# Decode attention with an MLP gate: TensorE in two two-round loops, w1 and V0 between the K halves, wide strip matmuls for the MLP output and three wo groups

## Chip, cores, metric

One Trainium2 chip, one core. The metric is device microseconds of one execution, lower is better. Each ratio below is the mean time of one kernel's fast runs over the mean of the other kernel's fast runs of the same rounds, so it is not quite the ratio of the medians that stand beside it. For a one-core kernel a run counts as "slow" when it is over 1.5% above the fastest run of the same kernel in the same comparison; the medians in the tables take in such runs, the ratios do not.

## The reference

Four batches, one token each, D = 512, 32 query heads in 8 groups, a cache of which the last 1024 positions count.

```python
def _A_ref(x, k_cache, v_cache, wq, wo):            # attention
    q = (x @ wq) -> (B, 32, 1, 128)
    k, v = last W = 1024 rows of the caches, each of 8 groups used by 4 heads
    p = softmax(q k^T * Dh**-0.5);  o = p v
    return o.reshape(B, 1, 4096) @ wo
def _B_ref(x, w1, b1, w2, b2):                      # MLP, 512 -> 1792 -> 512
    return gelu(layernorm(x) @ w1 + b1) @ w2 + b2

xn = layernorm(x)
s  = _A_ref(xn, k_cache, v_cache, wq, wo)
g  = silu(_B_ref(xn, w1, b1, w2, b2))
return x + s * g                                    # bf16 inputs and output
```

(Shortened. The weights and caches are some 28.8 MB, read once.)

## The kernel before

Each of the 8 K groups (1 MB) is transposed on TensorE in four units of eight 128x128 tiles, copied to SBUF by VectorE, and multiplied with q. V follows, group by group, then the product with wo. All TensorE code is written out: there is no loop. Loads go through SyncE in program order, and a load into a used slot waits for the last reader of that slot.

```python
NS, LAG, NKT, NB = 8, 8, 10, 3
d_wq = [load_wq(0)]; load_k(0); load_k(1); d_wq.append(load_wq(1))
for g in range(2, HKV): load_k(g)                   # kv_buf has 8 slots: all of K fits
...
def load_v(g):                                      # V goes into the slots of K
    dma(kv_buf[:, (HKV + g) % NS], cache_rows(A_v_cache, g), t_last[(HKV + g) % NS])
...
for n in range(LAG, NUN + LAG):                     # NUN = 32 units
    if n < NUN: T(n)                                # 8 transposes, copy to kt_buf
    S(n - LAG)                                      # 8 score matmuls, exp after the 4th
load_v(0); d_w1 = ...; load_v(1); d_w2 = ...
for g in range(HKV):
    if g >= 2: load_v(g)
    if g == 4: d_wox = ...                          # 128 rows of wo in a freed part of wq_sb
    PV(g)                                           # 32 matmuls and one for the denominator
    if g == 0: epilogue(0); mlp1()
    if g >= 2: epilogue(g - 1)
    if g == 1: mlp2(); mlp3()                       # MLP output: 56 narrow matmuls, early
    if g == 2: mlp4()
epilogue(HKV - 1)
... load_wo in pieces of 1 MB, 1, 1, 0.5, 0.25, 0.125

def wo(tiles, *deps):                               # "narrow": weights are 128x128 of wo,
    for w, o, st, sp in tiles:                      # the moving side has 4 columns
        for c in range(4):
            pe.matmul(psM[:, PS_W + c*4 : PS_W + (c+1)*4], w[:, c*128:(c+1)*128], o, ...)
rows = to_rows()
wo(wox...); for each wo piece: wo(...); gate; transpose; add x; store
```

The softmax here doesn't subtract the row's maximum and nothing guards it: scores larger than these inputs give would overflow.

Of the kernel before, what the change touches and what calls it, by code (L numbers as in the profile page):

```python
# [4 lines left out]
class _Op:  # L5
    __slots__ = ("eng", "fn", "deps", "sem", "count", "used")

    def __init__(self, eng, fn, deps, sem=None):
        self.eng = eng
        self.fn = fn  # L10
        self.deps = [d for d in deps if d is not None]
        self.sem = sem
        self.count = 0
        self.used = False


class _Program:



    ENGS = ("pe", "dve", "act", "gp", "sp")

    def __init__(self, nc):
        self.nc = nc
        self.ops = {e: [] for e in self.ENGS}
        self.sems = {e: nc.alloc_semaphore("e_" + e) for e in self.ENGS}

    def add(self, eng, fn, *deps):
        op = _Op(eng, fn, deps)
        self.ops[eng].append(op)  # L30
        return op

    def dma(self, eng, name, fn, *deps):
        op = _Op(eng, fn, deps, sem=self.nc.alloc_semaphore("d_" + name))
        self.ops[eng].append(op)
        return op

    def plan(self):
        for e in self.ENGS:
            for op in self.ops[e]:  # L40
                for d in op.deps:
                    if d.eng != e or e != "pe":
                        d.used = True
        for e in self.ENGS:
            n = 0
            for op in self.ops[e]:
                if op.sem is None:
                    if op.used:
                        n += 1
                    op.count = n  # L50

    def emit(self, e, engine):
        seen = {}
        for op in self.ops[e]:
            need = {}
            for d in op.deps:
                if d.sem is not None:
                    need[d.sem.name] = (d.sem, 16)
                elif d.eng != e or e != "pe":
                    s = self.sems[d.eng]  # L60
                    if need.get(s.name, (s, 0))[1] < d.count:
                        need[s.name] = (s, d.count)
            for name, (s, v) in need.items():
                if seen.get(name, 0) < v:
                    engine.wait_ge(s, v)
                    seen[name] = v
            last = op.fn(engine)
            if op.sem is not None:
                last.then_inc(op.sem, 16)
            elif op.used:  # L70
                last.then_inc(self.sems[e], 1)


def bass_recurrent_scan__sliding_block_cached__mixer_channel_mlp__decode_kernel(
# [20 lines left out]
    B, D = 4, 512  # L95
# [10 lines left out]
    NS = 8  # L106
    LAG = 8
    NKT = LAG + 2
# [17 lines left out]
    wox_sb = wq_sb[0:44, 0, 0:6 * D].rearrange("p (j o) -> p j o", j=6)  # L126
# [24 lines left out]
    ident32 = sb([128, 128], F32)  # L151
    ind = sb([128, 128], BF16)
# [6 lines left out]
    qT = sb([128, 128], BF16)  # L159
# [5 lines left out]
    selx = sb([128, 6, 44], BF16)  # L165
    OW3 = sb([128, 12], BF16)
    OWx = sb([44, 24], BF16)
# [18 lines left out]
    pg = _Program(nc)  # L186
# [18 lines left out]
    def load_k(g):  # L205
        d_k[g] = pg.dma("sp", "k%d" % g, lambda e: e.dma_start(
            kv_buf[:, g, :, :].rearrange("p c d -> p (c d)"), cache_rows(A_k_cache, g)),
            )

    def load_v(g):  # L210
        d_v[g] = pg.dma("sp", "v%d" % g, lambda e: e.dma_start(  # L211
            kv_buf[:, (HKV + g) % NS, :, :].rearrange("p c d -> p (c d)"), cache_rows(A_v_cache, g)),
            t_last[(HKV + g) % NS] if HKV + g >= NS else None)

# [6 lines left out]
    d_wq = [load_wq(0)]  # L221
    load_k(0)
    load_k(1)
    d_wq.append(load_wq(1))
    for g in range(2, HKV):
        load_k(g)
# [30 lines left out]
    c_sx = add("gp", lambda e: e.memset(selx[:, :, :], 0.0))  # L257
    for h in range(2):
        c_sx = add("gp", lambda e, h=h: e.affine_select(
            selx[:, 0:5, 32 * h:32 * h + 12], ones_bf[:, 0:60], [[1, 5], [5, 3], [15, 4]],  # L260
            ALU.is_equal, 0.0, base=60 * h, channel_multiplier=-1), c_1, c_sx)
    c_sx5 = add("gp", lambda e: e.affine_select(
        selx[:, 5, 0:8], ones_bf[:, 0:8], [[1, 8]], ALU.is_equal, 0.0,
        base=120, channel_multiplier=-1), c_1, c_sx)
# [22 lines left out]
    cp = {}  # L287
    sc = {}
    ex = [None] * HKV
    den = [None] * HKV  # L290
    ep = [None] * HKV

    def T(n):
        g, u = n // NU, n % NU

        def fn(pe):
            last = None
            for j in range(UT):
                last = pe.transpose(psK[n % NB][:, j * 128:(j + 1) * 128],  # L299
                                    kv_buf[:, g, u * UT + j, :], ident[:, :])  # L300
            return last
        t = add("pe", fn, d_k[g], c_id, cp.get(n - NB), v_xyT if n >= LAG else None)
        if u == NU - 1:
            t_last[g] = t
        cp[n] = add("dve", lambda e: e.tensor_copy(kt_buf[:, n % NKT, :], psK[n % NB][:, 0:1024]),  # L305
                    t, sc.get(n - NKT))

    def S(n):
        g, u = n // NU, n % NU

        def fn(pe):
            last = None
            if u == 0:
                pe.matmul(psS[g % 2][:, 0:512], ind[:, :], negm[:, :], start=True, stop=False,  # L314
                          skip_group_check=True)
            for j in range(UT):
                c = u * UT + j
                last = pe.matmul(psS[g % 2][:, c * 16:(c + 1) * 16],  # L318
                                 kt_buf[:, n % NKT, j * 128:(j + 1) * 128],
                                 qT[:, g * 16:(g + 1) * 16],  # L320
                                 start=False, stop=(c == NC - 1), skip_group_check=True)
            return last
        sc[n] = add("pe", fn, cp[n], v_q, c_neg, c_ind,
                    ex[g - 2] if u == 0 and g >= 2 else None)
        if u == NU - 1:
            ex[g] = add("act", lambda e: e.activation(  # L326
                P_buf[:, g, :], psS[g % 2][:, 0:512], AF.Exp, scale=SCALE),
                sc[n])

    def PV(g):  # L330
        pso = psO[g % 2]

        def fn(pe):
            last = None
            for c in range(NC):
                last = pe.matmul(pso[:, 0:16], kv_buf[:, (HKV + g) % NS, c, :],  # L336
                                 P_buf[:, g, c * 16:(c + 1) * 16],
                                 start=(c == 0), stop=(c == NC - 1))
            return last
        pv_op[g] = add("pe", fn, ex[g], d_v[g], ep[g - 2] if g >= 2 else None)  # L340

        den[g] = add("pe", lambda pe: pe.matmul(psS[g % 2][:, 0:512], ones_bf[:, :], P_buf[:, g, :],  # L342
                                                start=True, stop=True),
                     ex[HKV - 2 + g % 2], ep[g - 2] if g >= 2 else None)

    def epilogue(g):
# [9 lines left out]
            pso[:, 0:16], rden[:, cs], ALU.mult), v, pv_op[g])  # L356


    v_xyT = None
    for n in range(LAG):  # L360
        T(n)

    def f_xy(pe):
        last = None
        for s, src in ((0, xn_bf), (16, y_bf)):
            for c in range(4):
                last = pe.transpose(psK[1][:, s + c * 4:s + c * 4 + 4],  # L367
                                    bass.AP(src, c, [[512, 4], [4, 128]]), ident[0:4, 0:4])
        return last
    t_xy = add("pe", f_xy, v_xn, v_y, c_id, cp[LAG - 1])  # L370

    v_xT = add("dve", lambda e: e.tensor_copy(
        xT[:, :, 0:4], psK[1][:, 0:16].rearrange("p (c b) -> p c b", c=4)), t_xy, c_xT)
    v_xyT = add("dve", lambda e: e.tensor_copy(
        yT[:, :, 0:4], psK[1][:, 16:32].rearrange("p (c b) -> p c b", c=4)), t_xy, c_yT)
# [16 lines left out]
    def f_qT(pe):  # L392
        last = None
        for k in range(8):
            last = pe.transpose(psK[1][:, k * 128:(k + 1) * 128],  # L395
# [4 lines left out]
    for k in range(2):  # L400
        v_q = add("dve", lambda e, k=k: e.tensor_copy(
            bass.AP(qT, k * 64, [[128, 128], [16, 4], [4, 4], [1, 4]]),
            bass.AP(psK[1], k * 512, [[1024, 128], [32, 4], [1, 4], [128, 4]])), t_qT)
# [6 lines left out]
    def f32k(n):  # L410

        return kt_buf[:, n, 0:2 * FS].bitcast(F32)
    hb = kt_buf[:, 4, 0:FS]
    h_ps = psK[0][:, 0:2 * FS].bitcast(F32)

    def mlp1():
# [12 lines left out]
        t = add("pe", fn, v_xyT, d_w1, d_b1, *[cp[n] for n in range(NUN - NB, NUN)])  # L429
# [17 lines left out]
    def mlp3():  # L447
        def fn(pe):
            last = pe.matmul(psM[:, PS_Z:PS_Z + 16], b2_sb[:, :],  # L449
                             bass.AP(ident, 0, [[128, 4], [1, 4], [0, 4]]),  # L450
                             start=True, stop=False, skip_group_check=True)
            for k in range(FC):
                for c in range(4):
                    last = pe.matmul(psM[:, PS_Z + c * 4:PS_Z + (c + 1) * 4],
                                     w2_sb[:, k, c * 128:(c + 1) * 128], hT[:, k, 0:4],
                                     start=False, stop=(k == FC - 1), skip_group_check=True)
            return last
        t = add("pe", fn, mlp["h"], d_w2, d_b2, c_id)
# [9 lines left out]
    NUN = HKV * NU  # L468
    for n in range(LAG, NUN + LAG):
        if n < NUN:  # L470
            T(n)
        S(n - LAG)
    load_v(0)
    d_w1 = pg.dma("sp", "w1", lambda e: e.dma_start(
        w1_sb[:, :, :], B_w1.rearrange("(p c) f -> p c f", c=4)))
    load_v(1)
    d_w2 = pg.dma("sp", "w2", lambda e: e.dma_start(
        w2_sb[:, :, :], B_w2.rearrange("(p c) o -> p c o", c=FC)))
    for g in range(HKV):
        if g >= 2:  # L480
            load_v(g)
        if g == 4:


            R3 = (7 * 512 + 384) * D
            d_wox = [pg.dma("sp", "wox%d" % h, lambda e, h=h: e.dma_start(
                wox_sb[32 * h:32 * h + 12, 0:5, :].rearrange("p j o -> p (j o)"),
                bass.AP(A_wo.tensor, R3 + 60 * h * D, [[5 * D, 3], [15 * D, 4], [1, 5 * D]])),
                t_q) for h in range(2)]
            d_wox.append(pg.dma("sp", "wox2", lambda e: e.dma_start(  # L490
# [143 lines left out]
```

## Time and profile before

| | before |
|---|---|
| time, median of 3 | 76.88 us (76.87 to 76.88) |
| profiled span | 75.0 us |
| last V load lands | 62.22 us |
| last wo load lands | 71.89 us |
| TensorE's last narrow matmul ends | 72.22 us |
| 16 KB instruction fetches of TensorE | 8 |

The table of windows cuts the span in stages: window, its length, busy time of each engine (PE, PEld, DVE, ACT, POOL) with its instructions, the clock granted to TensorE, the DMA share, and GB/s. Of the kernel before:

```profile
33.00:47.00 14.00, 11.69 (x270) 9.53 (x269) 7.79 (x13) 2.99 (x5) 0.00 (x0) 0.94 1.00 423
47.00:63.00 16.00, 11.30 (x289) 8.24 (x287) 10.82 (x24) 1.31 (x3) 0.00 (x0) 0.50 1.01 423
```

The last column is what to read: 423 GB/s in both stages, with every other engine idle part of the time. The DMA sets the time until the last wo piece lands, and TensorE finishes 0.33 us after it. So a change must leave the queue fed and TensorE's tail under the last landing, or it costs time.

### The profile page before, as it was taken

The numbers are of one execution on the slowest core, as the hardware profiler recorded it, in microseconds if no ns is written. First come the engines' busy times: TensorE is split into PE (matmuls) and PEld (weight loads), VectorE is DVE, ScalarE is ACT, GpSimd is POOL, SyncE is SP. The second block draws the span as 40 slices with busy tenths as digits, with TensorE's granted clock in tenths as the row PEclk, the third lists the DMA queues.
The fourth block names the chain that finished last, engine by engine and source line by source line (L and its number), as shares of the span: only waits on it lengthen the run. The fifth ranks groups of instructions, "written<-read, shape, count | busy, mean of one in ns | idle before, by whom it ended". The sixth has DMA issues, their size and how long they took to land.

```text
span 75.0 us, 2384 instructions
## 1 busy us (share of the span) xinstructions
PE 49.1 (66%) x1089; PEld 40.3 (54%) x1089; DVE 41.2 (55%) x84; ACT 9.7 (13%) x16; POOL 7.2 (10%) x19
## 2 busy tenths in 40 slices
PE   0000029965689999959979937910899977379670
PEld 0000029953279989959979902500886555268640
DVE  0778106894258989959977060269639774620020
ACT  0611000000270320303203600230000000000000
POOL 6999300000000000000000000000000000000000
PEclk9999999999999999999999995555555555555555
DMA  1999999998999999999999999999999999999800
GB/s 37 271 413 420 417 420 476 437 420 376 433 437 433 415 433 420 424 415 464 419 398 425 461 413 401 424 420 428 419 429 428 420 409 420 417 411 419 322 25 2
DMA packets 4266, 28.99 MB, mean 387 GB/s; under 512 B 508, under 2 KB 648, under 8 KB 1697
## 3 DMA queue, kind: packets, MB, share of 16 engines
q1 hardware_dynamic: 4206, 28.84, 92.6%
q8 instruction: 8, 0.13, 0.6%
q10 hardware_dynamic: 50, 0.01, 0.1%
q14 instruction: 2, 0.01, 0.0%
HBM read 28.85 MB, written 0.00 MB: 385 GB/s over the span
## 4 chain that ended last, share of the span: by engine, by line
DMA 39%; PE 34%; SPq 15%; DVE 5%; issue 3%
DMA wo_sb<-in_A_wo_dram 26%; PE psK L299 20%; SPq L510 14%; DMA kv_buf<-in_A_k_cache_dram 13%; PE psS L318 6%; DVE kt_buf L305 4%; PE psO L383 3%; PE psS L314 2%; PE psM L555 2%; DVE q_sb L389 1%; PE psK L395 1%; PE psK L367 1%; PE psS L576 1%; SPq L218 1%; SPq L211 0%
## 5 line engine op out<-in xcount | busy, mean ns | idle before, releaser
L299 PE MATMUL psK<-ident,kv_buf 128*128 128x128 bf16 x256 | 20.5, 231 | 11.9 <-DMA kv_buf<-in_A_k_cache_dram 10.7
L305 DVE COPY kt_buf<-psK 128x1024 bf16<-128x1024 bf16 x32 | 21.1, 691 | 7.4 <-PE psK L299 7.3
L299 PEld LDWEIGHTS psK<-ident,kv_buf 128*128 128x128 bf16 x256 | 16.3, 104 | 11.3 <-DMA kv_buf<-in_A_k_cache_dram 10.7
L318 PEld LDWEIGHTS psS<-qT,kt_buf 128*128 128x128 bf16 x256 | 9.4, 96 | 2.1 <-issue 1.2
L318 PE MATMUL psS<-qT,kt_buf 128*128 128x16 bf16 x256 | 10.4, 169 | 0.2 <-issue 0.2
L336 PEld LDWEIGHTS psO<-P_buf,kv_buf 128*128 128x128 bf16 x256 | 7.5, 103 | 3.4 <-DMA kv_buf<-in_A_v_cache_dram 1.8
L336 PE MATMUL psO<-P_buf,kv_buf 128*128 128x16 bf16 x256 | 8.0, 174 | 0.9 <-DVE den_sb L349 0.7
L349 DVE TENSOR_REDUCE den_sb<-psS 128x16 f32<-128x512 f32 x8 | 5.5, 687 | 5.1 <-PE psS L342 4.9
L326 ACT ACTIVATE P_buf<-psS 128x512 bf16<-128x512 f32 x8 | 4.8, 597 | 16.2 <-PE psS L318 16.2
L555 PE MATMUL psM<-OW,wo_sb 128*128 128x4 bf16 x124 | 4.1, 167 | 0.8 <-DMA wo_sb<-in_A_wo_dram 0.8
L342 PE MATMUL psS<-P_buf,ones_bf 128*128 128x512 bf16 x8 | 4.5, 561 | 0.0
L555 PEld LDWEIGHTS psM<-OW,wo_sb 128*128 128x128 bf16 x124 | 3.7, 105 | 1.1 <-DMA wo_sb<-in_A_wo_dram 0.9
L572 DVE TENSOR_TENSOR sg_sb<-psM,g_sb 128x16 f32<-128x16 f32 x1 | 0.2, 185 | 5.8 <-PE psM L555 5.8
L421 PE MATMUL psK<-w_sb,yT 128*32 128x448 bf16 x16 | 2.0, 561 | 1.8 <-issue 1.8
L314 PE MATMUL psS<-negm,ind 128*128 128x512 bf16 x8 | 3.0, 380 | 0.0
L449 PE MATMUL psM<-ident,b_sb 4*128 4x16 bf16 x1 | 0.2, 190 | 3.8 <-DVE hT L444 3.8
L431 DVE SCALAR_TENSOR_TENSOR kt_buf<-kt_buf,psK 128x448 f32<-128x448 f32 x1 | 0.6, 622 | 3.7 <-ACT kt_buf L430 3.7
L449 PEld LDWEIGHTS psM<-ident,b_sb 4*128 4x128 bf16 x1 | 0.1, 99 | 4.3 <-DVE hT L444 4.3
L390 ACT ACTIVATE q_sb<-psO 128x512 bf16<-128x512 f32 x1 | 0.6, 597 | 13.1 <-PE psO L383 13.1
L267 DVE CAST P_buf<-x_bf 4x512 f32<-4x512 bf16 x1 | 1.0, 956 | 2.2 <-DMA x_bf<-in_A_x_dram 2.2
L352 DVE RECIPROCAL rden<-den_sb 128x16 f32<-128x16 f32 x8 | 2.0, 253 | 0.3
L440 DVE TENSOR_TENSOR kt_buf<-kt_buf,psK 128x448 bf16<-128x448 f32 x1 | 2.1, 2083 | 0.0
(74 smaller groups left out, 36.0 us busy)
## 6 DMA issues: line engine op xcount, KB each, us to landing
kv_buf<-in_A_k_cache_dram SPq DMA_DIRECT2D x8, 1024.0 KB, 20.6
kv_buf<-in_A_v_cache_dram SPq DMA_DIRECT2D x8, 1024.0 KB, 24.0
wq_sb<-in_A_wq_dram SPq DMA_DIRECT2D x2, 2048.0 KB, 11.4
w_sb<-in_B_w_dram SPq DMA_DIRECT2D x2, 1792.0 KB, 28.3
wo_sb<-in_A_wo_dram SPq DMA_DIRECT2D x3, 1024.0 KB, 24.0
wo_sb<-in_A_wo_dram SPq DMA_DIRECT2D x1, 512.0 KB, 19.6
wo_sb<-in_A_wo_dram SPq DMA_DIRECT2D x1, 256.0 KB, 16.4
wo_sb<-in_A_wo_dram SPq DMA_DIRECT2D x1, 128.0 KB, 14.6
```

What stands on the lines that cost most here:

```text
L299: last = pe.transpose(psK[n % NB][:, j * 128:(j + 1) * 128], kv_buf[:, g, u * UT + j, :], ident[:, :])
L305: cp[n] = add("dve", lambda e: e.tensor_copy(kt_buf[:, n % NKT, :], psK[n % NB][:, 0:1024]), t, sc.get(n - NKT))
L314: pe.matmul(psS[g % 2][:, 0:512], ind[:, :], negm[:, :], start=True, stop=False, skip_group_check=True)
L318: last = pe.matmul(psS[g % 2][:, c * 16:(c + 1) * 16], kt_buf[:, n % NKT, j * 128:(j + 1) * 128], qT[:, g * 16:(g + 1) * 16], start=False, ...
L326: ex[g] = add("act", lambda e: e.activation(P_buf[:, g, :], psS[g % 2][:, 0:512], AF.Exp, scale=SCALE), sc[n])
L336: last = pe.matmul(pso[:, 0:16], kv_buf[:, (HKV + g) % NS, c, :], P_buf[:, g, c * 16:(c + 1) * 16], start=(c == 0), stop=(c == NC - 1))
L342: den[g] = add("pe", lambda pe: pe.matmul(psS[g % 2][:, 0:512], ones_bf[:, :], P_buf[:, g, :], start=True, stop=True), ex[HKV - 2 + g % 2] ...
L349: v = add("dve", lambda e: e.tensor_reduce(den_sb[:, cs], bass.AP(psS[g % 2], 0, [[512, 128], [1, 16], [16, NC]]), AX.X, ALU.add), den[g])
L383: last = pe.matmul(psO[m // 4][32 * s:32 * s + 32, 0:512], xT[:, c, :], wq_sb[:, c, m * 512:(m + 1) * 512], start=(c == 0), stop=(c == 3), ...
L440: v = add("dve", lambda e: e.tensor_tensor(bass.AP(kt_buf, 4 * UT * 128, [[NKT * UT * 128, 128], [1, 32], [32, FC]]), f32k(3).rearrange("p ...
L510: d_wo.append((g0, g1, i0, i1, pg.dma("sp", "wo%d" % n, lambda e: e.dma_start(wo_sb[:, g0:g1, i0:i1, :], wo_r[:, g0:g1, i0:i1, :]))))
L555: last = pe.matmul(psM[:, PS_W + c * 4:PS_W + (c + 1) * 4], w[:, c * 128:(c + 1) * 128], o, start=(st and c == 0), stop=sp, skip_group_che ...
```

## The change

The intent: TensorE's written-out code is about 2,290 instructions, by an estimate nine blocks: the trace before shows fetches of 16 KB, and between its first four stalls for them lie 127 or 128 matmuls with as many weight loads, so some 256 instructions a block. The fetches move beside the data: after the first, at 24.3 us, fifteen increments of a K load came by 25.32 us and the sixteenth at 26.48. Two hardware loops of two rounds each, 4 K groups a round and 4 V groups a round, and wide matmuls in the tail bring it to about 1,330. In a loop of this program both rounds use the same slots, semaphores and buffers, hence the rest: K uses slots 0 to 3 twice, V slots 4 to 7 twice, w1 and V0 are loaded between the K halves, the softmax weights of groups 4 to 7 are copied into those of 0 to 3 by ScalarE, and the MLP output stands after the V loop.

```diff
-    d_wq = [load_wq(0)]
-    load_k(0)
-    load_k(1)
-    d_wq.append(load_wq(1))
-    for g in range(2, HKV):
+    d_wq = [load_wq(0), load_wq(1)]
+    for g in range(NG):                                    # NG = 4
         load_k(g)
 ...
     def load_v(g):
-            kv_buf[:, (HKV + g) % NS, ...], cache_rows(A_v_cache, g)),
-            t_last[(HKV + g) % NS] if HKV + g >= NS else None)
+            kv_buf[:, NG + g % NG, ...], cache_rows(A_v_cache, g)),
+            pv_op[g - NG] if g >= NG else None, sem=d_v[g - NG].sem if g >= NG else None)
 ...
+                with pe.Fori(0, 2, 1):                      # K loop and V loop
+                    for op in ops: ...
+    for r in range(2):
+        pg.seg = ("k", r)
+        if r:
+            d_w1 = ...
+            load_v(0)
+            for g in range(NG, HKV):
+                load_k(g)
+        for n in range(RU + LAG): ...                       # RU = 16, LAG = 3
+    load_v(1); d_w2 = ...; load_v(2); load_v(3)
+    mlp1()
     for g in range(HKV):
-        if g >= 2:
+        pg.seg = ("v", g // NG)
+        if g >= NG:
             load_v(g)
         PV(g)
+        epilogue(g)
 ...
-            for k in range(FC):                             # MLP output: 56 narrow matmuls
-                for c in range(4): ...
+            for k in range(FC):                             # 14 wide ones on four strips
+                i, m = k % 4, 32 if k < 4 else 4
+                last = pe.matmul(psK[1][32 * i:32 * i + m, ...], hT[:, k, 0:m],
+                                 w2_sb[:, k, :], ..., tile_position=(0, 32 * i))
+        mlp["zc"] = add("act", lambda e: e.activation(f32r(5), z_ps, AF.Copy), t)
+    def folded(pe, src, o, first, last):                    # sums the strips, and transposes
+        for c in range(4):
+            r = pe.matmul(psM[:, o + c * 4:o + (c + 1) * 4], src[:, c * 128:(c + 1) * 128],
+                          fold[:, :], ...)                  # src and fold are FP32
 ...
     rows = to_rows()
-    wo(wox: 6 tiles) ; wo(groups 0 to 6)
+    mlp3b()                                                 # fold of the MLP output
+    mlp4()
+    wide(groups 0 to 2: 12 matmuls of 512 columns); wide(wox: 2)
+    w_c = add("act", lambda e: e.activation(f32r(6), psK[2][...], AF.Copy), t_w)
+    add("pe", lambda pe: folded(pe, f32r(6), PS_W, True, False), w_c, c_fold, mlp["g"])
+    wo(groups 3 to 6)
```

(Not in this excerpt: the bookkeeping of semaphores that a loop needs; the layout of the extra 128 wo rows, "wox", which changes from 40 KB on three DMA engines to 16 KB on eight, which the traces show as three data increments in each of its two large transfers before and eight after; wo pieces of 1.5, 1, 0.5, 0.5, 0.25 and 0.125 MB.)

## The prediction

> **What bounds the kernel now.** I read the page first (busy shares, slices, queues), then the chain of work that ended last, the timeline of the tail, the timeline around TensorE's "issue" gaps, and last the trace's record of when each of a DMA's sixteen increments arrived. The page's slices and queues:
>
> ```profile
> PE   0000029965689999959979937910899977379670
> PEclk9999999999999999999999995555555555555555
> DMA  1999999998999999999999999999999999999800
> GB/s 37 271 413 420 417 420 476 437 420 376 433 437 433 415 433 420 424 415 464 419 398 425 461 413 401 424 420 428 419 429 428 420 409 420 417 411 419 322 25 2
> ...
> q1 hardware_dynamic: 4206, 28.84, 92.6%
> q8 instruction: 8, 0.13, 0.6%
> ```
>
> The DMA row is 9 from the second slice to the 38th at about 420 GB/s, while TensorE has gaps. 28.84 MB must be moved, and neither kernel moves fewer data bytes. The clock row says that TensorE has half its clock from about 45 us on. The chain of work that ended last says the same of its second half:
>
> ```profile
> 51.25 0.04 issue
> 51.30 19.64 DMA wo_sb<-in_A_wo_dram
> 70.93 0.05 issue
> 70.98 0.59 PE psM L555 x16
> 71.57 0.04 issue
> 71.61 0.61 PE psM L555 x12
> 72.22 0.02 issue
> 72.24 0.20 DVE sg_sb L572
> ```
>
> The last 28 narrow matmuls run as the last wo pieces land (71.89 us is the last increment); then come 3.1 us of product, transpose, sum and output to the end at 75.0. The timeline of the tail shows how little room TensorE has there:
>
> ```profile
> 66.51 0.88 PE L555 MATMUL psM<-OWx,wq_sb 44*128 44x4 bf16 x24 [0.53 <-DVE OWx L547]
> 67.33 1.87 PE L555 MATMUL psM<-OW,wo_sb 128*128 128x4 bf16 x64
> 69.73 1.01 PE L555 MATMUL psM<-OW,wo_sb 128*128 128x4 bf16 x32 [0.54 <-DMA wo_sb<-in_A_wo_dram]
> 70.98 1.23 PE L555 MATMUL psM<-OW,wo_sb 128*128 128x4 bf16 x28 [0.23 <-DMA wo_sb<-in_A_wo_dram]
> ```
>
> Its waits for DMA there are 0.54 + 0.23 = 0.77 us: TensorE may grow by about 0.8 us after 66.5 before it, and not DMA, sets the end.
>
> The second reading is of **instruction fetches**. In the trace eight 16 KB packets of the instruction queue start at 24.3, 30.8, 36.8, 43.0, 49.2, 57.7, 64.9 and 70.1 us, each taking 0.88 to 0.97 us. TensorE stops for "issue" soon after the first four:
>
> ```profile
> 33.08 0.22 PE L299 MATMUL psK<-ident,kv_buf 128*128 128x128 bf16 x1 [0.81 <-issue]
> 45.48 0.56 PE L421 MATMUL psK<-w_sb,yT 128*32 128x448 bf16 x4 [1.81 <-issue]
> ```
>
> These gaps lie 127 matmuls apart, which with their weight loads and a wait or two is 256 instructions = 16 KB. Each ends 1.3 to 1.5 us after the packet, and the next packet starts 3.7 to 4.2 us after the gap. So one block is fetched ahead, only once the block before it is entered, and it takes about 4 + 0.95 + 1.35 = 6.3 us under this load. That costs TensorE some 3.3 us in the K stage, but the bytes flow on.
>
> A fetch also delays one of the sixteen DMA engines by 1.2 to 1.4 us to the end. The fifth K load got fifteen increments by 25.32 us, the sixteenth at 26.48; every fetch up to the seventh adds one late engine. The last wo piece has five increments at 70.25 to 70.57, one at 71.05, ten at 71.53 to 71.89 (seven with a fetch, and the three engines that carry 40 KB each of the extra wo rows: those two transfers show three data increments each); the mean is 71.29. **Perfect balance is worth 0.6 us, no fetches at all about 1.3.** Two per cent of 76.88 is 1.54.
>
> [...] no line of this trace shows whether old blocks stay usable. [...] The change hangs on which holds. [...] the 32 q matmuls of 128x512 take 1.91 us, 60 ns each at full clock. [...] The change adds FP32 matmuls with 128-column weights; the kernel before has one such only with 16 columns.
>
> **The change part by part.**
>
> Loops. Sixteen units of transpose and score are 260 matmuls, 520 instructions, some 535 with waits: over two blocks. V: 4 x 33 matmuls, some 280 instructions. With the narrower tail TensorE's code falls from about 2,290 to about 1,330 instructions, nine blocks to six. If old blocks stay, fetches fall from eight to about five: 0.05 MB, 0.1 us of DMA on average. But the last engine still has one fetch on it, so the last landing moves only 0.1 or 0.2 us. The V copies on ACT (8 x 0.6 us at most; ACT is 13% busy) and the register work lie beside.
>
> DMA order. wq entire first: its second half lands at 13.1 instead of 18.0; K3 at 22.9; w1 and V0 (2.9 MB at 0.43 MB a us) hold 6.9 us; K4 lands at 32.2, K7 at 39.7. After V1, w2, V2, V3 and the wox rows, the queue is fed until about 51.9, so V4 must be issued by about 50, and it now waits for V0's products. Transpose plus score takes 0.65 us a unit (2.8 us a group). Starting at 32.2 and half cold, the second K round ends at 44 to 45, w1 products at 46.5, V0's at 48: in time by 2 us. No gain, as the bytes are the same.
>
> Tail. V7 lands at about 62.1 as before, and its products end at 63.7. Then, at half clock: 14 strip matmuls for the MLP. Four of 448 columns took 0.37 us a round (L421), so 512 columns 0.43; four rounds with drain 1.7, of which 1.3 lie beside the epilogue on DVE (to 65.0): 65.3. Row products 0.8: 66.1. Fold of the MLP, four FP32 matmuls and a bias: I estimate 0.3 us each, from the one FP32 transpose here that took 383 ns against about 220 for bf16: 1.3, so 67.4. Wide matmuls for three groups and wox, four rounds plus drain: 1.9, so 69.3. ACT copy 0.6 with a hand-over of 0.1: 70.0. Second fold 1.2: 71.2. Groups 3 to 6, 64 narrow ones at 29 ns: 1.9. Last 12: 0.4 and drain. End about 73.6, against 72.24 before: **+1.3 us**. It removes 24 + 48 narrow ones, 2.1 us, but puts two folds, a copy and wide ones in the chain. With folds half as dear, or TensorE warm, it ends with the DMA at 72.1.
>
> Sum where old blocks stay: -0.1 for DMA, 0 to +1.3 for the tail: 76.8 to 78.1.
>
> **The rivals.**
>
> Old blocks do not stay [...]. Then the K loop's back branch waits 6.3 us for its first block and again for following ones, and the V loop too: 12 or 13 fetches. The 6.9 us of w1 and V0 would hide the first stall; that they stand just there speaks for the author expecting one. But the first block has only about 80 body instructions, 2 us of work, so another 4 us wait follows, then over 1 us per block. K would end at 50 to 54, V0's products at 55 or later, and V4 would be issued 4 us after the queue ran dry. The V back branch would put another 6 to 12 us in front of V4's products. That makes 80 to 88 us. For it: the gaps before, a fetch on demand each time. Against it: [...] that a loop would save no fetch then. I give it a third.
>
> Balance. If fetches vanish or avoid the engines that carry wox (now 16 KB on eight engines, 0.6 us, instead of 40 KB on three), the last landing comes up to 1.0 us earlier: 75.9. If they hit the same engines, 0.5 later. It cannot reach 2%.
>
> TensorE warm in the tail: then +0. Before, it stayed at half clock from 45 us with 7 tenths busy, which speaks against.
>
> **Range and chances.** About two thirds on 76.0 to 78.5, centred a little above the present time; a third on 80 and beyond, wide. The median of that mixture is about 77.4 us. 76.0 to 83.0 leaves a twentieth below and some 15% above. Faster by over 2%: 0.04, as no term reaches 1.54 us. Slower: nearly all of the third and a little of the rest, 0.36. Within: 0.60.
>
> **What would show it.** Right: the instruction queue with about five packets; no "issue" gap of over 1 us at the start of the second K and V rounds; DMA row at 9 to the 38th slice; last wo increment at 71.5 to 72.0; TensorE's last narrow matmuls without waits for DMA, later than 72.24. [...] I am wrong if the last landing comes a full 1.5 us earlier, if FP32 folds take over 0.6 us each, or if a wait on a slot (V4 on V0's products) starves the queue without any fetch gap.

## The result, and the profile after

The changed kernel is slower. In the first comparison it took 79.95 us median (78.76, 79.58, 80.33 and 81.27; the latter two count as slow) against 76.88; ratio of fast runs 1.0294, interval 1.0201 to 1.0387. In a later one it took 80.59 (80.25 to 81.0, six runs, all fast) against 76.80; ratio 1.0501, interval 1.0475 to 1.0526. The profile below is that of the 78.76 us run. It is the fastest run, for a reason that its clock row shows. Its page:

```profile
PEclk9999999999999999965999999999555555598555
GB/s 36 248 419 426 470 452 358 422 434 434 417 476 395 409 441 400 443 422 426 422 434 433 463 400 411 430 329 374 396 405 417 415 407 422 422 413 399 116 9 2
q8 instruction: 5, 0.08, 0.4%
PE psM L561 4%; PE psM L670 3%; PE psK L552 2%; PE psK L683 1%; PE psO L426 1%; ACT kt_buf L697 1%; ACT kt_buf L557 1%; PE psS L433 1%; PE psS L712 1%; DVE o_bf L714 0%; DVE sg_sb L708 0%; PE psM L567 0%
```

Five fetches instead of eight (q8). A dip in the GB/s row, 329 374 396, in the middle of the V stage. And a chain that ended last (fourth line) with no DMA in it, as far back as it is followed (to 63.36 us): before, wo's DMA stood in it until 70.93 us. The clock row has "98" in slices 36 and 37 of 40: in this run TensorE got its full clock for one stretch of 3.4 us, from 67.2 us on.

**The loops fetch once.** The fetches begin at 23.0, 29.1, 51.3, 68.4 and 73.8 us: two in the first K round, none in the second, though a round has 128 transposes and 128 score matmuls, each with a weight load, which are 512 instructions without the waits; one in the first V round, none in the second. The back edge costs a branch of 0.22 us (0.08 where not taken), in the trace's records of the K and of the V loop. The timeline has a gap at the start of the second K round, and its releaser is TensorE's sequencer:

```profile
33.60 3.32 PE L387 MATMUL psK<-ident,kv_buf 128*128 128x128 bf16 x32 [4.10 <-PEq L99]
```

It is no fetch. The last increment of K4 arrived at 33.47, 0.13 us before; the wait for it is given to the instruction of the loop that waits. Fourteen of K4's sixteen increments were there by 32.08, the last two came at 33.46 and 33.47. After the first fetch one increment of w1 came late (28.60, the others by 27.17), after the second two of V0 (31.03 and 31.18, the others by 29.64), and two of each load from K4 to V1. So the two fetches of the first K round seem to start the second one 1.4 us later; this is read from the increments, and no run tests it.

**A hole before V4.** TensorE and SyncE around it, the timeline first, then the waits of the DMA queue (line waited for: us in total, times, longest):

```profile
47.26 0.94 PE L518 MATMUL psK<-w_sb,yT 128*32 128x448 bf16 x16 [0.78 <-ACT P_buf L415]
48.13 0.37 PE L522 MATMUL psK<-b_sb,ones_bf 1*32 1x448 bf16 x4
48.43 1.99 PE L426 MATMUL psO<-P_buf,kv_buf 128*128 128x16 bf16 x64
...
56.22 0.94 PE L426 MATMUL psO<-P_buf,kv_buf 128*128 128x16 bf16 x29 [2.21 <-DVE OTb L448]
```

```profile
SPq L294 <- PE psO L426: 17.6, 2, 16.4
```

V4's load waits in SyncE for V0's products (L426), and is issued at 49.42 us, when those 32 matmuls end. The queue had V3 (increments from 50.72 to 52.38) and wox (51.07 to 53.40) left, unevenly over its engines. The trace's packet records, which no view prints, show the hole: from about 50.4 us engines stand empty, between 50.5 and 51.0 some 11 of the sixteen are busy and move 0.27 MB a us, and V4's first packets start at 50.88, 1.5 us after the issue. The rate is back above 0.42 MB a us only at 58, though most engines are busy by then; why it stays low so long is not shown. V4's first increment arrives at 54.16, its last at 55.82, 4.74 and 6.40 us after the issue. TensorE then waits 2.2 us for V4 (the page names VectorE, which came last by its record; V4's last increment at 55.82 is what fits). The windows give the loss:

```profile
33.00:47.00 14.00, 12.66 (x256) 12.26 (x260) 10.57 (x16) 2.28 (x4) 0.00 (x0) 0.88 1.01 427
47.00:63.00 16.00, 9.08 (x247) 6.98 (x251) 10.47 (x23) 3.53 (x7) 0.00 (x0) 0.71 0.98 398
```

398 against 423 GB/s over 16 us is 0.40 MB, or 0.95 us. V7's last increment is at 63.27 us instead of 62.22, wo's at 73.18 instead of 71.89.

How late V4 is issued goes with the clock of the second K round, in which TensorE is busy for over 12 of 14 us. In the window from 33 to 47 us the mean granted clock is 0.88 here and in the profiles of e1, e5 and e11, and V4 is issued at 49.42 to 49.58 us; in those of e2, e3, e4 and e6 it is 0.79 to 0.82, and V4 is issued at 50.04 to 50.36. V7 then lands at 62.90 to 63.62 us in the first four and at 63.99 to 64.28 in the others. That of e3, to set beside the first line above:

```profile
33.00:47.00 14.00, 13.35 (x256) 12.68 (x257) 10.67 (x16) 1.79 (x3) 0.00 (x0) 0.81 1.01 428
```

**A longer tail.** The timeline of TensorE in the tail, from the profile of the later comparison (80.95 us, half clock throughout the tail):

```profile
65.29 1.89 PE L552 MATMUL psK<-w_sb,hT 128*32 128x512 bf16 x14
66.67 0.62 PE L644 MATMUL psS<-OTb,sel 128*32 128x28 bf16 x16
...
68.00 1.87 PE L561 MATMUL psM<-fold,kt_buf 128*128 128x4 f32 x8
69.80 1.47 PE L683 MATMUL psK<-wo_sb,OW 128*32 128x512 bf16 x12
71.20 0.59 PE L683 MATMUL psK<-wq_sb,OWx 64*4 64x512 bf16 x2
72.47 1.87 PE L561 MATMUL psM<-fold,kt_buf 128*128 128x4 f32 x8 [0.69 <-ACT kt_buf L697]
74.20 2.17 PE L670 MATMUL psM<-OW,wo_sb 128*128 128x4 bf16 x76
```

wo's last increment is at 73.27 us here. TensorE ends at 76.37, 3.1 us after it, and nothing in this list waits for DMA. Each fold (L561), four FP32 matmuls in the program, stands as eight pairs of weight load and matmul and takes 1.87 us; such a weight load took a median of 333 ns here, against 106 in e11, where the folds are BF16. In the 78.76 us run the same lines are 1.06, 0.83, 0.38 and 1.71 us:

```profile
67.63 1.06 PE L561 MATMUL psM<-fold,kt_buf 128*128 128x4 f32 x8
68.61 0.83 PE L683 MATMUL psK<-wo_sb,OW 128*32 128x512 bf16 x12
69.38 0.38 PE L683 MATMUL psK<-wq_sb,OWx 64*4 64x512 bf16 x2
70.44 1.71 PE L561 MATMUL psM<-fold,kt_buf 128*128 128x4 f32 x8 [0.69 <-ACT kt_buf L697]
```

So the tail of this kernel is TensorE's and moves with the clock, and it spreads from 78.8 to 81.3 us, where the kernel before, whose tail is the DMA's, stays at 76.7 to 77.0. Of its ten runs in both comparisons the two with the highest mean clock (0.848 and 0.845) are the two fastest (78.76 and 79.58 us); the other eight, at 0.786 to 0.821, are not in the order of their clocks. The profiles show two places where the clock acts, this stretch of 3.4 us and the second K round; which of them made each run is not on record.

### The profile page after: what moved, and what is told of

It reads as the page before. It is cut to its first block, busy times and chain, and to the rows that moved or that the text cites. A ratio compares the mean times of both kernels' runs of the same rounds, so it can differ in the third digit from the quotient of the medians.

```text
span 76.9 us, 2253 instructions
## 1 busy us (share of the span) xinstructions
PE 49.6 (64%) x989; PEld 40.8 (53%) x1001; DVE 40.4 (53%) x85; ACT 13.1 (17%) x22; POOL 7.6 (10%) x23
## 5 line engine op out<-in xcount | busy, mean ns | idle before, releaser
L387 PEld LDWEIGHTS psK<-ident,kv_buf 128*128 128x128 bf16 x256 | 17.3, 108 | 4.2 <-issue 4.2
L426 PE MATMUL psO<-P_buf,kv_buf 128*128 128x16 bf16 x256 | 7.9, 172 | 7.2 <-PEq L99 4.7
L426 PEld LDWEIGHTS psO<-P_buf,kv_buf 128*128 128x128 bf16 x256 | 7.3, 100 | 8.8 <-issue 4.6
L407 PE MATMUL psS<-qR,kt_buf 128*128 128x16 bf16 x256 | 10.5, 170 | 0.4
L407 PEld LDWEIGHTS psS<-qR,kt_buf 128*128 128x128 bf16 x256 | 9.6, 96 | 1.1
L475 PE MATMUL psO<-wq_sb,xT 128*32 128x512 bf16 x32 | 3.8, 628 | 2.9 <-DMA wq_sb<-in_A_wq_dram 2.7
L481 DVE CAST q_sb<-psO 128x512 bf16<-128x512 f32 x1 | 0.7, 691 | 6.5 <-PE psO L475 6.5
L475 PEld LDWEIGHTS psO<-wq_sb,xT 128*32 128x32 bf16 x32 | 0.9, 129 | 5.0 <-DMA wq_sb<-in_A_wq_dram 3.6
L561 PE MATMUL psM<-fold,kt_buf 128*128 128x4 f32 x16 | 2.8, 296 | 0.7 <-ACT kt_buf L697 0.7
L561 PEld LDWEIGHTS psM<-fold,kt_buf 128*128 128x128 f32 x16 | 2.6, 247 | 1.0 <-ACT kt_buf L697 1.0
L437 ACT ACTIVATE P_buf<-P_buf 128x512 bf16<-128x512 bf16 x4 | 2.4, 621 | 2.0 <-PE psS L433 1.3
L670 PEld LDWEIGHTS psM<-OW,wo_sb 128*128 128x128 bf16 x76 | 2.3, 106 | 0.0
```

Of the source, the lines that this page charges most:

```text
L387: last = pe.transpose(psK[n % NB][:, j * 128:(j + 1) * 128], kv_buf[:, lg, u * UT + j, :], ident[:, :])
L407: last = pe.matmul(psS[lg % 2][:, c * 16:(c + 1) * 16], kt_buf[:, n % NKT, j * 128:(j + 1) * 128], qR[:, lg * 16:(lg + 1) * 16], start=Fal ...
L426: last = pe.matmul(pso[:, 0:16], kv_buf[:, NG + lg, c, :], P_buf[:, lg, c * 16:(c + 1) * 16], start=(c == 0), stop=(c == NC - 1))
L437: pc[lg] = add("act", lambda e: e.activation(P_buf[:, lg, :], P_buf[:, NG + lg, :], AF.Copy), den[g], cls="pc")
L475: last = pe.matmul(psO[m // 4][32 * s:32 * s + 32, 0:512], xT[:, c, :], wq_sb[:, c, m * 512:(m + 1) * 512], start=(c == 0), stop=(c == 3), ...
L561: r = pe.matmul(psM[:, o + c * 4:o + (c + 1) * 4], src[:, c * 128:(c + 1) * 128], fold[:, :], start=first and c == 0, stop=last, skip_grou ...
```

## The experiments

The theory: two things cost time, the late issue of V4 (a hole in the DMA) and the FP32 folds in TensorE's tail; the loops themselves cost and gain nothing. Rivals: the loops (branches, waits, semaphore work) cost it; the loss is all DMA; the loss is elsewhere in the order of loads. All kernels gave correct results. Slow by the 1.5% rule were three of the four runs of e2, one of six in e5 and in e6, and two of six in e11.

| run | median us (range, runs) | before beside it | ratio, 95% interval |
|---|---|---|---|
| e1 the change, again | 80.59 (80.25–81.0, 6) | 76.80 | 1.0501, 1.0475–1.0526 |
| e2 loops written out | 81.03 (79.11–81.16, 4) | 76.80 | none (one fast run) |
| e3 wide wo undone | 78.55 (78.27–79.38, 6) | 76.80 | 1.0248, 1.0210–1.0286 |
| e4 a wo piece ahead of V4 | 81.21 (81.1–81.45, 4) | 76.80 | 1.0578, 1.0560–1.0596 |
| e5 both wide forms undone | 78.37 (77.79–78.97, 6) | 76.83 | 1.0198, 1.0157–1.0238 |
| e6 e5 with a wo piece ahead | 78.32 (77.73–79.78, 6) | 76.83 | 1.0156, 1.0126–1.0186 |
| e7 V4–V7 in K's slots | 79.27 (79.18–80.33, 6) | 76.83 | 1.0341, 1.0298–1.0384 |
| e8 the K loop alone | 77.31 (77.07–77.6, 6) | 76.83 | 1.0068, 1.0049–1.0087 |
| e9 before, with wide wo | 77.88 (77.86–78.76, 5) | 76.80 | 1.0152, 1.0128–1.0175 |
| e10 e8, wox laid out as before | 76.74 (76.62–76.89, 6) | 76.80 | 0.9989, 0.9974–1.0004 |
| e11 folds in BF16 | 78.49 (78.11–80.02, 6) | 76.80 | 1.0199, 1.0168–1.0230 |
| e12 e7 with folds in BF16 | 77.14 (76.73–77.24, 6) | 76.80 | 1.0033, 1.0011–1.0055 |

e1 to e4 ran on one chip, e5 to e8 on a second, e9 to e12 on a third. Across those, only the ratios to the kernel before are compared.

### e1: the changed kernel again

No edit.

> The changed kernel unaltered, as a control. Theory A: the 2 to 4 us that it loses come from two places, (1) V4 waits for the slot that V0's products free, so the DMA queue runs dry for about 1 us at 50 to 54 us, and (2) a serial TensorE chain after V7 lands (11 us: products, MLP strips, row products, fold, wide wo, copy, fold, 76 narrow matmuls) that outlasts the DMA. Both depend on the TensorE clock, [...] so the time spreads from run to run: 78.7 to 81.5 us, while the kernel before stays within 76.8 to 77.1 on the same chip. Rival (noise of the earlier chip): this one repeats within 0.3% too.

Measured 80.59 us, ratio 1.0501. All six runs lie within 0.75 us, where the slower half of the first comparison lies too, so 80 to 81 us is read as this kernel's usual time and the 78.76 us run as the exception. This is the tail shown above.

### e2: the same order with the loops written out

```diff
-            if not isinstance(seg, tuple):
+            if True:                                        # no loop; own semaphores for K4-7, V4-7
                 for op in ops:
```

> The changed kernel with TensorE's two loops written out straight, each transfer with its own semaphore, nothing else changed. Theory A (the loops themselves are harmless, and spare fetches): no gain, 78.7 to 82 us, with about 7 or 8 packets in the instruction queue in place of 5, issue gaps in the K stage again, and V4 issued no earlier than 49.4 us, rather 1 to 2 us later. Rival B (branches, semaphore lowering or refetched blocks of the loops cost the time): 77.5 us or less and the tail as short as before.

Measured 81.03 us. Three of four runs are at 81.0 to 81.2, with a mean clock of 0.785 to 0.802, and one at 79.11 with 0.846. The profile, which by the 1.5% rule counts as slow beside that one run, has eight fetches again; V4 is issued at 50.24 us, TensorE's folds take 1.87 us each, and wo lands at 73.92. With one fast run there is no verdict; but no run came near the 77.5 us of the rival, and the late V4 and the long tail are there without loops. So nothing here says that the loops cost the time, and three fetches fewer do not show as a gain either. For the K loop e10 is the firmer test; the V loop has no other than this.

### e3: wide matmuls for wo undone

```diff
-    wide(groups 0 to 2); t_w = wide(wox); w_c = copy; folded(w_c)
-    for g0, g1, i0, i1, d in d_wo[1:]:
+    wo(wox: 2 tiles)
+    for g0, g1, i0, i1, d in d_wo:                          # all groups narrow
```

> The changed kernel with the wide wo matmuls, their copy and the second fold undone: all of wo in narrow matmuls, MLP output still in strips with its fold. Theory A: the stretch from the first wide matmul to the start of the 76 narrow ones (68.6 to 72.2, 3.55 us) becomes 56 narrow ones at 29 ns (1.6 us), so the chain is about 1.9 us shorter and the DMA sets the end again: last wo increment near 73.2, TensorE done 0.35 us later, 0.7 us off the profiled run and more off the slow ones: 77.8 to 78.4 us, and less spread. Rival C (the tail is set by DMA, the wide form lies beside it): no change, 78.7 to 80.

Measured 78.55 us, ratio 1.0248 against 1.0501 of the unaltered change on the same chip: 2.0 us gained by undoing one wide form, with more matmuls (124 narrow ones instead of 76, and 8 for wox). In its profile V4 was issued at 50.20 us and V7 landed at 64.18, later than in e1 (the slower second K round shown above), and it is still faster. The wide form with its copy and fold is a loss where TensorE is the tail.

### e4: a wo piece issued ahead of V4

```diff
+        if g == NG:
+            load_wo(2, 5, 6, 0, 4)                          # 512 KB that wait for no slot
         if g >= NG:
             load_v(g)
```

> The changed kernel with one 512 KB piece of wo (group 5) issued ahead of V4, so that it fills the hole in the queue. Theory A: the GB/s row has no hole at 50 to 54 us any more, the last wo increment comes about 1.0 us earlier (72.2), V7 lands at about the same time (63.2 to 63.5), and as the TensorE chain starts from V7 the time stays within 0.3 us of the changed kernel. Rival D (the hole alone makes the loss): 1.0 us faster, 77.7 or so.

The GB/s row has no hole any more, and the last wo increment comes at 72.44 us, 0.8 us before that of e1. The time does not fall: 81.21 us. V4 still waits for V0's products and is issued at 50.04, after a slow second K round (clock 0.82), and V7 landed at 63.99, as it did in e2 and e3 at that clock without the piece (64.05 and 64.18). The tail follows V7:

```profile
GB/s 68 305 414 404 430 470 367 437 420 437 416 455 411 419 420 425 412 445 412 441 438 425 411 437 412 413 411 396 412 429 412 414 420 418 416 263 13 0 8 2
```

```profile
72.84 1.87 PE L561 MATMUL psM<-fold,kt_buf 128*128 128x4 f32 x8 [0.69 <-ACT kt_buf L700]
74.57 2.17 PE L673 MATMUL psM<-OW,wo_sb 128*128 128x4 bf16 x76
```

So the total of DMA idle time is not what costs; what costs is when V7 lands plus the chain behind it. "All DMA" has fallen.

### e5 and e6: both wide forms undone, without and with the piece ahead

```diff
-            for k in range(FC): ... 14 strip matmuls, copy, fold
+            for k in range(FC):
+                for c in range(4): ... 56 narrow matmuls, after the V loop
     (and the edit of e3; e6 adds the edit of e4)
```

> The changed kernel with both strip forms undone: MLP output and all of wo in narrow matmuls as before the change, no fold; loops and DMA order kept. Theory A: the TensorE chain after V7 now ends before the data, so the last wo increment plus 0.35 us ends TensorE. What is left against the kernel before is the hole in the queue alone (1.2 to 2.2 us by how late V4 is issued): 77.8 to 78.6 us, some 0.4 us under the run with only wo narrow. Rival (the chain is still the bound): under 0.2 us of gain over that run.

> The same, and one 512 KB piece of wo issued ahead of V4. The same move gained nothing in the changed kernel, where the chain sets the end. Theory A: here it does gain, as DMA sets the end: last wo increment near 72.4, 77.1 to 77.6 us, within 1% of the kernel before. Rival (the hole costs nothing): as the run before this, 77.8 to 78.6.

e5 took 78.37 us, e6 78.32, where 77.1 to 77.6 had been expected of e6: a miss. The trace of e6 shows why. The narrow tail has more instructions, and a fetch now stops TensorE within it:

```profile
69.28 1.14 PE L675 MATMUL psM<-OW,wo_sb 128*128 128x4 bf16 x37
71.57 2.46 PE L675 MATMUL psM<-OW,wo_sb 128*128 128x4 bf16 x87 [1.14 <-issue]
```

The fetch begins at 69.17 us; TensorE stands still for 1.14 us. The tail also starts late: in this profile V4 was issued at 50.36 and V7 landed at 64.28, against 49.58 and 62.90 in that of e5. e5 has the same stall (1.11 us at 70.16), but waits for DMA afterwards anyway (0.56 us), so there it does not set the end: its last wo lands at 73.33, TensorE ends at 73.65. With the folds gone, the hole remains.

### e7: the hole removed, and the V loop with it

V is written straight instead of looped, all eight softmax weights are kept, and V4 to V7 go into the slots of K4 to K7, which are free by then. So the ScalarE copies of the weights go too; they are not tested alone.

```diff
-            kv_buf[:, NG + g % NG, ...], ..., pv_op[g - NG] if g >= NG else None
+            kv_buf[:, (NG + g) % NS, ...], ..., t_last[g] if g >= NG else None
...
-        pg.seg = ("v", g // NG)
+        pg.seg = "mid"
```

> The changed kernel with the V loop written out straight and V4 to V7 put into the K slots, which are free from 36 us on, so no V load waits for products; the strip forms and folds of the tail stay. Theory A: no hole, V7 lands at 62.2 in place of 63.6, last wo increment near 72; the chain of 12.8 us after V7 at half clock then ends at 75.0: about 79.4 us, 1.1 to 1.4 faster than the changed kernel at half clock, still 2.5 slower than the kernel before. Rival (DMA alone is at fault): 76.9.

Measured 79.27 us (79.4 was expected), ratio 1.0341. No hole: 421 GB/s in the window from 47 to 63 us, V7 at 62.80, wo at 72.49. TensorE still ends at 75.32, 2.8 us after the last landing, with both folds at 1.87 us.

### e8 and e10: the K loop alone

e8 is e7 with the narrow tail, and with the MLP output at V3, ahead of the tail. e10 lays wox out as the kernel before does.

```diff
 e8  -    mlp3() after V7, wide ; wide wo
     +        if g == 3: mlp3()                             # narrow
     +        if g == 4: mlp4()
 e10 -    wox_sb = wq_sb[0:64, 0, 0:2 * D]                  # 16 KB on eight engines
     +    wox_sb = wq_sb[0:44, 0, 0:6 * D]                  # 40 KB on three
```

> As the run before, and the tail as in the kernel before the change (MLP output narrow after V3's products, all wo narrow): only the K loop and the new DMA order are left of the change. Theory A: as fast as the kernel before, 76.6 to 77.0 us, with 6 or 7 instruction packets. Rival (the K loop or the order w1, V0 between the K halves costs something itself): over 77.3.

> The run with the K loop alone (V straight, V4 to V7 in the K slots, narrow tail), with the last 128 rows of wo laid out as in the kernel before: 40 KB on three DMA engines instead of 16 KB on eight. Theory 'balance' (that run's last landing, 72.51 against 71.89, is late because fetches of instructions fell on engines that also carry those rows): last landing 71.8 to 72.0 and 76.6 to 76.9 us, level with the kernel before. Rival (the K loop or the order of V0 and w1 costs it): 77.2 to 77.5 us, as that run.

e8 took 77.31 us, 0.3 to 0.7 above its expectation: a miss. Its last wo increments come in steps: five by 70.43 us, five more by 70.99, four by 71.91, then 72.35 and 72.51. That suggested that fetches (by the prediction's reading of the increments each delays one engine, by 1.2 to 1.4 us) fell on engines that carry wox as well (0.6 us by the prediction's estimate). e10 tested it and met its numbers: the sixteen increments are now seven by 70.36 and nine from 71.10 to 71.99, with nothing later, and the time is 76.74 us, level with the kernel before (0.9989). Its tail waits for DMA, as the tail before did:

```profile
67.86 2.72 PE L676 MATMUL psM<-OW,wo_sb 128*128 128x4 bf16 x96
71.09 1.22 PE L676 MATMUL psM<-OW,wo_sb 128*128 128x4 bf16 x28 [0.50 <-DMA wo_sb<-in_A_wo_dram]
72.59 0.38 PE L710 MATMUL psS<-ident,sg_sb 128*16 128x128 f32 x1 [0.28 <-DVE sg_sb L706]
```

So the K loop, LAG of 3 (scores follow transposes by 3 units, not 8), wq in one go, and w1 and V0 between the K halves cost nothing, and with six fetches instead of eight (e8's page) gain nothing (ratio 0.9989). That the fetches hit the very engines of wox is read from the increments; no view names the engine of a fetch, so the cause of those 0.5 us is supported, not shown directly.

### e9: the wide form of wo put into the kernel before

```diff
+    t_w = add("pe", wide, d_wo[0][4], rows[0])             # groups 0 to 2, 12 matmuls
+    w_c = add("act", copy to FP32, t_w)
+    add("pe", folded, w_c, c_fold)                         # FP32
-    for g0, g1, i0, i1, d in d_wo:
+    for g0, g1, i0, i1, d in d_wo[1:]:
```

(Not in this excerpt: the first wo pieces become 1.5, 1, 0.5 and 0.5 MB, as in the changed kernel.)

> The kernel before with only the wide form of wo groups 0 to 2: twelve strip matmuls, the ScalarE copy and an FP32 fold in place of 48 narrow matmuls. Theory A (the tail form costs TensorE time at half clock, and wo's last landing no longer hides it): 48 narrow (1.4 us) go, wide 1.47, copy 0.7 and fold 1.87 come, so TensorE ends near 73.4 instead of 72.2: 77.7 to 78.2 us, 1.0 to 1.4 above the kernel before. Rival (the form lies beside the DMA's last landings, as the prediction had it): 76.7 to 77.0 us.

Measured 77.88 us, 1.08 us over the kernel before, in the middle of what the theory said. wo's last increment is where it was (71.97 us), so the loss is TensorE's: 48 narrow matmuls, 1.4 us, became 1.47 + 0.70 + 1.87 us, of which part goes into the 0.77 us that TensorE had idle. (The profiled run is the slowest of the five, 78.76 us: in it V7's products also began 0.9 us later.)

### e11 and e12: the folds in BF16

```diff
-    fold = sb([128, 4], F32)
+    fold = sb([128, 4], BF16)
-        e.activation(f32r(5), z_ps, AF.Copy)               # likewise the second copy
+        e.activation(kt_buf[:, 5, 0:512], z_ps, AF.Copy)   # BF16
```

e11 is the changed kernel with this alone; e12 has the edit of e7 too, so both named causes are gone. (The strips are rounded to BF16 before they are summed; the result still passes.)

> The changed kernel with both folds in BF16 (fold constant and copied strips; rounding differs slightly). Theory A (the FP32 folds, 1.87 us each at half clock, are the mis-sized term of the tail): about 3 us less on TensorE's chain, which then ends near the last landing of 73.2 to 73.4: 77.6 to 78.5 us, and a narrower spread over runs. Rival (the folds matter little, the hole before V4 is all): less than 1 us gained, over 79.3 us.

> The changed kernel with V written straight, V4 to V7 in the K slots, and both folds in BF16: both named causes are taken away. Theory A: the chain ends near 72.1 to 72.5, so the DMA's last landing of about 72.5 sets the end: 76.9 to 77.5 us, level with the kernel before or half a microsecond over it. Rival (something else in the change costs): over 78 us.

e11: 78.49 us, at the upper edge of what was expected. Its fold is 0.27 us, and its tail waits for DMA again, at a last landing of 73.35 us:

```profile
70.39 0.27 PE L561 MATMUL psM<-fold,kt_buf 128*128 128x4 bf16 x4 [0.69 <-ACT kt_buf L697]
70.52 1.42 PE L670 MATMUL psM<-OW,wo_sb 128*128 128x4 bf16 x48
72.47 1.19 PE L670 MATMUL psM<-OW,wo_sb 128*128 128x4 bf16 x28 [0.54 <-DMA wo_sb<-in_A_wo_dram]
```

e12: 77.14 us, ratio 1.0033, all six runs within 0.5 us. In the chain that ended last the DMA stands again where the folds stood:

```profile
55.70 16.27 DMA wo_sb<-in_A_wo_dram
71.96 0.05 issue
72.01 0.61 PE psM L666 x12
```

The two causes account for all but 0.3%. Against the kernel before, the change is +5.0% (e1), without the folds' cost +2.0% (e11), without the hole +3.4% (e7), without both +0.3% (e12). These ratios are from three chips, and the change's own differs between comparisons (1.029 and 1.050), so the shares, about 2.3 us for FP32 and 1.2 us for the hole, are rough. The firm parts: e11 against e12, on one chip, for the hole (fast runs 78.11 to 78.73 against 76.73 to 77.24 us), and e7 against e12, on two chips with the kernel before at 76.83 and 76.80, for the folds (ranges 1.9 us apart).

No version beats the kernel before; e10 matches it.

## Why the prediction was right or wrong

The range (76.0 to 83.0) holds the result, but that is luck, for the argument is only half right: the class with the highest chance, within 2%, did not come, and the 79.95 us fall in the gap between its two scenarios. The upper part of the range, and most of the 0.36 for "slower", were there for a rival that did not happen.

**Right: no gain, and the fetches.** "If old blocks stay, fetches fall from eight to about five" and no stall of over 1 us from a fetch at the back edges: five came, and one branch costs 0.22 us. The rival in which old blocks do not stay, given a third, expected 12 or 13 fetches and is refuted: five packets here, none of them in the second K or V round, five in e1 and eight in e2. "It cannot reach 2%" faster held, down to e10.

**Right in kind, wrong in size: the tail.** The prediction had TensorE's chain from V7's landing (62.1) to the last narrow matmul (73.6) at 11.5 us. In e1 it is 63.62 to 76.37, or 12.75 us. Term by term at half clock: landing to the end of V7's products 1.6 predicted, 1.74 measured; then to the start of the MLP fold 2.4 against 2.64; MLP fold 1.3 against 1.80; wide matmuls 1.9 against 2.0; copy 0.7 against 0.67; second fold 1.2 against 1.73; narrow ones 2.4 against 2.17 (starts taken from line to line). **The mis-sized term is the FP32 fold**, "I estimate 0.3 us each, from the one FP32 transpose here that took 383 ns against about 220 for bf16": that transpose stands in the trace as one weight load and one matmul (L576 before, L712 after), but each FP32 matmul of the fold as two, and eight starts in 1.73 us are 0.43 us for each of the four. Four BF16 calls took 0.27 us in all in e11, four FP32 calls 1.87. The line "I am wrong ... if FP32 folds take over 0.6 us each" did catch it only if read of the whole fold.

**Wrong: "in time by 2 us".** The prediction put V0's products at 48, the end of the queue's work at 51.9 and so V4's deadline at "about 50". All that lead was lost, on both sides. The products ended at 49.4 us: the second K round took about 13 us, as expected, but began at 33.6, not 32.2, for it had to wait for the two late increments of K4. The prediction had measured that a fetch holds up one engine by 1.2 to 1.4 us, and did not put this into its landing times. And the first engines were empty at 50.4, not 51.9; with the measured 1.5 us from issue to first packets the deadline was 48.9. That made V7 land at 63.3 to 63.6 instead of 62.1: 1.2 to 1.5 us more in front of the same tail (and some 0.7 us more where the clock in the second K round was lower). Of this the hole is 0.95 us by bytes; V7 lands at 62.60 and 62.80 in e12 and e7, where it is closed, so about 0.5 us has another cause, perhaps the uneven load of the engines (62.33 in e10, with wox on three). The prediction did list it, "if a wait on a slot (V4 on V0's products) starves the queue without any fetch gap", as what would make it wrong, and that is what happened.

The sum: +1.5 us (V7) and +1.25 us (tail) on 73.6 give the measured 76.37. "Last wo increment at 71.5 to 72.0" failed likewise: 73.2.

**Balance.** "If they hit the same engines, 0.5 later" agrees in size with e8 against e10 (72.51 against 71.99 us), and the hoped-for "75.9" did not appear in any run. "No fetches at all about 1.3" does not follow from the prediction's own increments: of the ten last ones, at 71.53 to 71.89 us, it gives seven to fetches and three to the engines that carry wox, and by that reading those three would still land late without fetches. No run tests it.

**Clock.** "TensorE warm in the tail: then +0" was set aside; it came in the profiled run, for one stretch of 3.4 us, and bears on the spread rather than the median.

## What to carry to other kernels

Before a load is made to wait on a slot, find the moment when the first DMA engine, not the last, runs out of work, put the deadline ahead of it by the time from an issue to its data, here 1.5 us, and check the last matmul that frees the slot against that, at the lowest clock that its stage gets. When DMA sets the end, look at how much idle time TensorE has behind the last dependent load, here 0.77 us, and price every instruction of a new tail at the clock that the tail gets, in a sequence and in its own data type (a fold took 1.87 us in FP32 and 0.27 in BF16, e1 and e11); fewer matmuls can be a longer chain (e3, with more of them, was 2.0 us faster). Saving instruction fetches saved nothing here (six instead of eight, and a ratio of 0.9989 in e10); one seems to matter where the increment that it delays is the one waited for, as at the start of the second K round, 1.4 us later by the increments.
